# Closing batch 0's attention early in a fused attention and MLP kernel

## The chip, the cores and the metric

The kernel runs on one core of one Trainium2 chip. The metric is the device time of one execution in microseconds (us). An execution is called fast when it lies within 1.5% of the fastest of the same kernel, and a difference counts as faster or slower from 2% on. Ratios are the mean time of one kernel's fast runs over the mean of the other's in the same rounds, so they are not quite the ratio of the medians quoted beside them.

Engines: PE is TensorE (PEld its weight loads), DVE is VectorE, ACT is ScalarE, POOL is GpSimd, SP is SyncE. SPq and ACTq are queues on which SP and ACT issue transfers. TensorE's clock is called warm where 512-column products follow each other every 0.216 us, and cold where they do so every 0.42 us (five warming products).

## The reference

Eight batches, eight heads, 576 positions, head width 64; attention with a causal mask and a decay bias, then a normalisation over the 512 channels and an MLP of width 2048 with a residual.

```python
def _attn_ref(q, k, v, s):
    scores = scale * np.matmul(q, k.transpose(0, 1, 3, 2))
    cum = np.cumsum(np.maximum(s, 0.0), axis=-1)
    bias = -(cum[:, :, :, None] - cum[:, :, None, :])
    scores = np.where(causal, -1000000000.0, scores + np.minimum(bias, 0.0))
    # ... softmax ...
    return np.matmul(attn, v)

def _moe_ref(x, g_ln, w_ch1, w_ch2):
    mu = np.mean(x, axis=-1, keepdims=True)
    var = np.mean((x - mu) ** 2, axis=-1, keepdims=True)
    xn = (x - mu) / np.sqrt(var + 1e-06) * g_ln
    return x + np.maximum(xn @ w_ch1, 0.0) @ w_ch2
```

The bias enters as four more rows under the 64 rows of q and k (the "bias rows"), so that one product gives scores with bias.

## The kernel before

The 64 heads run in one loop. Head n's scores (q times k) are followed by the PV product (softmax weights times V) of an earlier head, and the MLP of batch b - 1 is cut into small units that fill TensorE while batch b's heads run. The PV result is drained by DVE. After a batch's last head, DVE aggregates the statistics and writes the normalised tiles `xn`; these are transposed on TensorE (`trx`) and copied to `xT`, from which the MLP starts.

```python
    def ln_aggr(b):
        n = len(x_tiles(b))
        mvs[b] = small.tile([P, 5, 2], F32, name="mv", tag="mv", bufs=2)
        for t in range(n):
            nc.vector.bn_aggr(out=mvs[b][:, t, :], in_=st[b][:, t, :, :])
    # ...
    def ln_xn(b):
        xTs[b] = xtp.tile([P, KD, 512], BF16, name="xT", tag="xT")
        for t, x in enumerate(x_tiles(b)):
            xn = xnp.tile([P, Dm], BF16, name="xn", tag="xn")
            nc.vector.scalar_tensor_tensor(
                out=xn, in0=x, scalar=mvs[b][:, t, 0:1], in1=gb,
                op0=ALU.subtract, op1=ALU.mult,
            )
            xns[b, t] = xn
    # ...
    def pv_next():
        pb, ph_ = pend.pop(0)
        pv(pb, ph_)
        if ph_ in (3, 5, 7):
            ln_stats(pb, ph_ // 2 - 1)
        if ph_ == 7:
            ln_aggr(pb)
            ln_xn(pb)
            ln_rstd(pb)
```

For the first three batches, k and q come in pairs of heads, are transposed on TensorE into PSUM (`trqk`) and copied from there (`qk_pair`). The loads that matter here stand in `pre(n)`, which runs ahead of head n. `ld_w1`, `ld_w2` and `ld_cast_pair` are issued by POOL, which also casts V:

```python
        elif n == 8:
            ld_cast_pair(6)
            ld_w2(1)
            cast_v(1, 0, "pool")
            cast_v(1, 1, "pool")
        elif n == 9:
            ld_w2(2)
            cast_v(1, 2, "pool")
            # ... V tiles 3 and 4
        elif n == 10:
            ld_cast_pair(7)
            ld_w2(3)
```

The softmax here doesn't subtract the row's maximum and nothing guards it: scores larger than these inputs give would overflow.

## Time and profile before

| | before |
|---|---|
| time, median (range) | 387.93 us (387.8 to 389.07), 3 runs |
| profiled span | 385.7 us |
| lost TensorE time, 0 to 50 us | 30.0 us |
| lost, 50 to 100 us | 7.2 us |
| lost, 310 to 320 us | 4.0 us |
| first MLP product | 45.53 us |
| head 63's scores begin | 299.78 us |

"Lost" is the length of the stretch less the columns of its matmuls at 2400 per us (narrow ones counted as 64), without the warming products; a product counts where it starts. It shows how far the stretch is from dense work, which busy time does not. The start of a head's first score product (`sa`) is a milestone: the same head in two kernels tells how far one is ahead. The main lines behind this table stand in the prediction.

### The profile page before, as it was taken

How to read it: one execution, taken by the hardware profiler on the slowest of the kernel's cores; microseconds unless marked ns; L12 is line 12 of the kernel's file. 1: busy time of each engine (PE TensorE's matmuls, PEld its weight loads, DVE VectorE, ACT ScalarE, POOL GpSimd, SP SyncE). 2: the span in 40 equal slices, each digit the busy share in tenths (PEclk: the TensorE clock that was granted, in tenths of full speed). 3: DMA queues.
4: the chain of work that ended last, by engine and by line, in shares of the span. 5: the costliest groups of instructions: out<-in, count | busy, mean ns of one | idle time of the engine just before them, and what ended most of it. 6: DMA issues, size and time to landing. Idle time of an engine off the chain costs nothing.

```text
span 385.7 us, 8249 instructions
## 1 busy us (share of the span) xinstructions
PE 363.9 (94%) x3016; PEld 197.3 (51%) x3016; DVE 202.5 (53%) x538; ACT 194.5 (50%) x366; POOL 161.6 (42%) x442
## 2 busy tenths in 40 slices
PE   7878798997999999999999999999999979999994
PEld 2556455555555555565555555555555534444442
DVE  7557747768644754484356536743665473212211
ACT  7768667673874377427733773376346401411410
POOL 5861377437473365535565563456742110000000
PEclk9889899999999999999999999999999989999999
DMA  8799996178795599759887996589620011002013
GB/s 199 126 182 195 210 168 128 24 167 166 165 186 121 129 229 202 169 132 216 185 202 184 204 191 163 140 200 210 152 97 0 2 56 54 1 29 82 0 34 77
DMA packets 147777, 51.86 MB, mean 134 GB/s; under 512 B 134140, under 2 KB 142936, under 8 KB 147736
## 3 DMA queue, kind: packets, MB, share of 16 engines
q1 hardware_dynamic: 139352, 44.18, 50.5%
q0 software_dynamic: 8384, 7.15, 12.2%
q8 instruction: 24, 0.39, 0.4%
q14 instruction: 17, 0.14, 0.1%
HBM read 37.11 MB, written 9.44 MB: 121 GB/s over the span
## 4 chain that ended last, share of the span: by engine, by line
PE 80%; DMA 8%; DVE 5%; ACT 3%; SPq 1%; issue 1%; POOL 0%; ACTq 0%; DVEq 0%; POOLq 0%
PE py L457 31%; PE ph L439 30%; DMA vtmp<-in_v_dram 7%; PE pot L352 6%; PE sc L276 3%; PE sb L276 3%; PE sa L276 3%; PE trx L426 2%; ACT er L287 2%; DVE xn L410 2%; ACT kq L96 1%; DMA pairtmp<-in_q_dram 1%; PE trqk L229 1%; DMA kq<-c 1%; DVE yo L466 1%
## 5 line engine op out<-in xcount | busy, mean ns | idle before, releaser
L457 PE MATMUL py<-w_bf,hT 128*128 128x512 bf16 x576 | 137.9, 381 | 2.5 <-DVE yo L466 2.2
L439 PE MATMUL ph<-xT,w_bf 128*128 128x512 bf16 x512 | 123.2, 382 | 1.2 <-DVE hT L447 1.0
L449 ACT ACTIVATE hT<-ph 128x512 bf16<-128x512 f32 x107 | 63.9, 598 | 85.5 <-PE ph L439 85.5
L439 PEld LDWEIGHTS <-w_bf 128*128 128x128 bf16 x576 | 52.0, 98 | 55.2 <-issue 6.0
L457 PEld LDWEIGHTS <-hT 128*128 128x128 bf16 x576 | 52.2, 98 | 52.8 <-issue 4.0
L287 ACT ACTIVATE er<-sa 128x512 bf16<-128x512 f32 x64 | 38.1, 596 | 71.6 <-PE sa L276 44.8
L295 POOL TENSOR_SCALAR_AFFINE_SELECT er<-er 128x128 bf16<-128x128 bf16 x216 | 58.4, 294 | 33.3 <-ACT er L287 33.3
L447 DVE TENSOR_SCALAR hT<-ph 128x512 bf16<-128x512 f32 x37 | 25.6, 691 | 58.0 <-PE ph L439 54.9
L163 POOL CAST rows<-rowtmp 128x512 bf16<-128x512 f32 (+1 forms) x50 | 30.4, 607 | 44.3 <-DMA rowtmp<-in_q_dram 39.9
L352 PEld LDWEIGHTS <-er 128*128 128x128 bf16 x960 | 38.3, 99 | 17.9 <-DVE xm L369 3.1
L276 PEld LDWEIGHTS <-kq 68*128 68x128 bf16 x440 | 32.8, 98 | 27.6 <-DMA kq<-c 2.5
L360 DVE RECIPROCAL rinv<-pot 128x5 f32<-128x5 f32 x64 | 12.4, 194 | 61.5 <-PE pot L352 61.3
L352 PE MATMUL pot<-v_bf,er 128*128 128x65 bf16 x960 | 40.6, 195 | 2.3 <-DVE xm L369 1.8
L287 ACT ACTIVATE er<-sc 128x512 bf16<-128x512 f32 x64 | 39.1, 611 | 0.0
L100 POOL CAST v_bf<-vtmp 128x512 bf16<-128x512 f32 (+1 forms) x40 | 24.6, 620 | 32.9 <-DMA vtmp<-in_v_dram 32.5
L287 ACT ACTIVATE er<-sb 128x512 bf16<-128x512 f32 x64 | 38.3, 598 | 0.0
L466 DVE SCALAR_TENSOR_TENSOR yo<-py,rstd,xb 128x512 f32<-128x512 f32 x32 | 23.8, 748 | 25.5 <-PE py L457 20.3
L96 ACT COPY kq<-trqk 64x576 bf16<-64x576 bf16 x28 | 22.5, 802 | 11.9 <-PE trqk L229 11.7
L362 DVE TENSOR_TENSOR xb<-pot,rinv 128x256 f32<-128x256 f32 x64 | 27.2, 425 | 2.2
L276 PE MATMUL sa<-kq 68*128 68x512 bf16 x64 | 24.6, 385 | 3.0 <-DMA kq<-c 2.4
L276 PE MATMUL sc<-kq 68*128 68x256 bf16 (+1 forms) x208 | 25.2, 232 | 0.2
L386 DVE BATCH_NORM_STATS2 stats<-xb 128x6 f32<-128x128 f32 (+1 forms) x96 | 25.0, 320 | 0.4
(93 smaller groups left out, 302.2 us busy)
## 6 DMA issues: line engine op xcount, KB each, us to landing
vtmp<-in_v_dram SPq DMA_DIRECT2D x32, 256.0 KB
out_dram<-yo SPq DMA_DIRECT2D x32, 256.0 KB
rowtmp<-in_k_dram SPq DMA_DIRECT2D x40, 128.0 KB
rowtmp<-in_q_dram SPq DMA_DIRECT2D x40, 128.0 KB
w_bf<-in_moe_w_ch_dram POOLq DMA_DIRECT2D x8, 512.0 KB, 11.1
kp<-in_k_dram POOLq DMA_DIRECT2D x10, 144.0 KB, 4.4
qp<-in_q_dram POOLq DMA_DIRECT2D x10, 144.0 KB, 5.1
vtmp<-in_v_dram SPq DMA_DIRECT2D x8, 128.0 KB
```

What stands on the lines that cost most here:

```text
L96: nc.scalar.copy(out=out, in_=in_)
L163: nc.gpsimd.tensor_copy(out=r[0:pn, :, :, 0:D], in_=loaded.pop(("rows", gam, t))[0:pn])
L276: nc.tensor.matmul(a[:, c + a0 - q0 : c + a1 - q0], lhsT=k_cols(b, h, kb), rhs=cols, start=True, stop=not (pe_mask and diag),)
L287: nc.scalar.activation(out=e[:, o : o + 512], in_=a, func=ACT.Exp, scale=scale)
L295: nc.gpsimd.affine_select(out=e[:, o : o + P], in_=e[:, o : o + P], compare_op=ALU.is_ge, fill=0.0, base=0, pattern=[[1, P]], channel_mult ...
L352: nc.tensor.matmul(pot[:, t, :], lhsT=e[:, o : o + P], rhs=vv[:, kb, h, :], start=(kb == 0), stop=(kb == last),)
L362: nc.vector.tensor_tensor(out=xb[b][:, :, hs], in0=pot[:, 0:NF, 0:D], in1=rinv[:, 0:NF].unsqueeze(2).to_broadcast([P, NF, D]), op=ALU.mult,)
L439: nc.tensor.matmul(ph, lhsT=w1_bf[:, kd, fb * P : (fb + 1) * P], rhs=xT[:, kd, :], start=(kd == 0), stop=(kd == KD - 1),)
L447: nc.vector.tensor_scalar_max(out=hT[:, fb, :], in0=ph, scalar1=0.0)
L449: nc.scalar.activation(out=hT[:, fb, :], in_=ph, func=ACT.Relu)
L457: nc.tensor.matmul(py[0], lhsT=hT[:, fb, t * P : (t + 1) * P], rhs=w2_bf[:, fb, :], start=(fb == 0), stop=(fb == FB - 1),)
L466: nc.vector.scalar_tensor_tensor(out=yo, in0=py[0], scalar=rs, in1=x, op0=ALU.mult, op1=ALU.add)
```

## The change

The intent is to begin the MLP sooner: batch 0's last three PV products are drained and normalised before batch 1 starts. The bias rows of the first heads come by broadcast transfer. Pair 1 no longer loads ahead of V. The end is shortened too. The core of the diff, cut:

```diff
@@ normalisation: one function for one tile, aggregate and xn in turn
-        for t in range(n):
-            nc.vector.bn_aggr(out=mvs[b][:, t, :], in_=st[b][:, t, :, :])
+    def ln_xn(b, t):
+        ...
+        nc.vector.bn_aggr(out=mvs[b][:, t, :], in_=st[b][:, t, :, :])
+        xn = xnp.tile([P, Dm], BF16, name="xn", tag="xn")
+        nc.vector.scalar_tensor_tensor(out=xn, in0=tiles[t], ...)
...
         if ph_ == 7:
-            ln_aggr(pb)
-            ln_xn(pb)
-            ln_rstd(pb)
+            ln_open(pb)
+            for t in range(NT if pb < B - 1 else 1):
+                ln_xn(pb, t)
@@ batch 0 closed after head 7
+            if n == 7:
+                pv_next()
+                tr_pair(4)
+                pv_next()
+                pv_next()
+                evac_pair("k", 4, ("act", "act"))
...
+        if n == 8:
...
+            for t in range(NF):
+                ln_tr(0, t, "act")
+            queue += batch_units(0)
+            run_units(3)
@@ loads
         elif n == 8:
-            ld_cast_pair(6)
             ld_w2(1)
-            cast_v(1, 0, "pool")
-            cast_v(1, 1, "pool")
         elif n == 9:
-            ld_w2(2)
-            cast_v(1, 2, "pool")
...
+            for t in range(NT):
+                cast_v(1, t, "pool")
+            ld_cast_pair(6)
         elif n == 10:
-            ld_cast_pair(7)
+            ld_w2(2)
             ld_w2(3)
...
+        elif n == 11:
+            ld_cast_pair(7)
@@ the end: last norm spread between units, its copies on ACT, last tile in halves
     for t in range(NT):
-        ln_tr(B - 1, t)
+        ln_xn(B - 1, t + 1)
         run_units(1)
+        ln_tr(B - 1, t, "act")
```

Not shown: the start's copies split over ACT and DVE, the transposes of the bias columns moved from head 14 to head 12 with half of their copies on ACT, pairs 7 to 10 transposed at heads 13 to 16, the PV product of head 7 in another PSUM buffer, and the number of MLP units per head, now computed from what is left in the queue.

## The prediction

> **What bounds the kernel now.** I read the page first, then the busy times by stage, then TensorE's waits, then the timeline where those waits stand. Of the page's slices (one is 9.64 us) these count:
>
> ```profile
> PE   7878798997999999999999999999999979999994
> ...
> PEclk9889899999999999999999999999999989999999
> DMA  8799996178795599759887996589620011002013
> ```
>
> TensorE is full from about 100 us to the end but for one dent near 315 us; the first five slices are 7s and 8s, and part of that is the kernel's own warming products. The stages, from the view by windows:
>
> ```profile
> 0.00:45.50 45.50, 35.00 (x370) 21.33 (x371) 31.26 (x82) 33.61 (x57) 23.46 (x44) 0.92 1.03 179
> 45.50:50.00 4.50, 4.13 (x28) 2.08 (x27) 0.69 (x1) 2.22 (x5) 2.29 (x5) 0.62 1.24 227
> ...
> 80.00:100.00 20.00, 17.69 (x170) 10.13 (x167) 14.24 (x39) 11.98 (x21) 11.68 (x32) 1.00 0.73 168
> 100.00:310.00 210.00, 209.92 (x1866) 116.59 (x1865) 115.56 (x333) 112.11 (x223) 104.10 (x312) 1.00 0.70 157
> 310.00:321.00 11.00, 8.75 (x48) 4.53 (x47) 7.18 (x19) 0.00 (x0) 1.16 (x1) 0.84 0.13 49
> ```
>
> The columns are PE, weight load, DVE, ACT, POOL, granted clock, DMA share, GB/s. Busy time flatters TensorE, so I count columns. Four 512-column products take 0.863 us in the timeline's dense stretches, 0.216 us each. In 0 to 45.5 us the products other than the 39 warming ones (groups by form) have 42,400 columns, 17.9 us at that rate: 27.6 us are lost. The same count gives 16.7 of 20 us in 80:100 (3.3 lost), 7.1 of 11 in 310:321 (3.9 lost), 8.1 of 10 in 60:70 (1.9 lost), and next to nothing in 100:310. So the total is TensorE's work plus these losses plus the tail. A loss removed comes off the end at full size, because everything after it is dense.
>
> Which waits are these? TensorE's waits in the first 130 us, longest first, are these (after 130 us one more counts: 2.2 us of py L457 for DVE yo L466, at 314.8 us):
>
> ```profile
> PE sa L276 <- DMA kq<-c: 2.4, 1, 2.4
> PE trqk L229 <- DVE xT L431: 2.1, 1, 2.1
> PE pot L352 <- DVE xm L369: 1.8, 2, 0.9
> PE trx L426 <- DVE xT L431: 1.7, 1, 1.7
> ```
>
> The first is head 4 waiting at 22.0 us for its bias rows; the clock then falls to half until 28.9 us. The second stands at 90.9 us: pair 10's transposes need a PSUM buffer that holds a transpose of batch 1's norm. Last, how the first MLP product is reached, and how the run ends:
>
> ```profile
> 38.20 0.64 PE L352 MATMUL pot<-v_bf,er 128*128 128x65 bf16 x15 [0.93 <-DVE xm L369]
> ...
> 40.20 3.26 ACT L96 COPY kq<-trqk 64x576 bf16<-64x576 bf16 x4 [2.12 <-PE trqk L229]
> ...
> 40.83 3.02 DVE L410 SCALAR_TENSOR_TENSOR xn<-xb,mv,gb 128x512 bf16<-128x512 f32 x4
> ...
> 43.84 1.64 DVE L431 COPY xT<-trx 128x512 bf16<-128x512 bf16 x4
> ...
> 45.53 1.55 PE L439 MATMUL ph<-xT,w_bf 128*128 128x512 bf16 x4
> ```
>
> ```profile
> 380.82 0.75 DVE L466 SCALAR_TENSOR_TENSOR yo<-py,rstd,xm 128x512 f32<-128x512 f32 x1 [2.70 <-PE py L457]
> 381.60 0.47 SPq L489 DMA_DIRECT2D out_dram<-yo  x1
> 382.12 0.59 SPq L490 DMA_DIRECT2D out_dram<-yo  x1
> ```
>
> Batch 0's last PV product starts at 38.2 us, and 7.3 us pass to the first MLP product: drain, statistics, four normalisations, then four copies on the same DVE. ACT meanwhile copies pair 5, and head 9's exponentials wait until 43.5 us.
>
> **What the Trainium skill says.** "Perfetto Trace Analysis", Identifying the Most-Contended Engine, says that matmul busy time is no measure of the distance to the roofline; the trace agrees (35.0 us busy, 17.9 us of columns). "TensorE: Matmul & The Clock Gate", What's actually happening, has the clock at half after an idle window of about 3.4 us; its section "Wait — 56ns, not 53.3ns?" puts 512 columns at 426.7 ns cold and 215.7 warm. The trace agrees: 0.216 us dense, and a granted clock of 0.62 in 45.5:50, just after the starved stretch. "DMA: Bandwidth & Descriptors", Anatomy of one DMA, has about 2.0 us of fixed cost per transfer. The first bias rows (4.5 KB or less) agree: last issue over at 11.7 us, used at 13.9. Its section Queues, rings and completion order has each engine alternate between queues by packet; so small rows queue with the weights, and the rows issued from 17.6 to 20.1 us landed only at 24.4.
>
> **The change part by part.**
>
> *Start.* Pair 1's k and q leave the first queue (two 288 KB loads), and the constant rows come by broadcast DMA in place of one 2.11 us ACT copy and the memsets. The first scores start at 12.14 us now. After it: k cast on ACT to 5.8, q cast on POOL (0.8 to 1.3 us) to about 7.2, then on ACT two k copies (0.81 each), the bias row (0.57) and two q copies. That gives about 10.4 us. The sync queue is blocked by V loads until 8.5 us now; with less ahead, the bias rows of heads 1 to 3 should land at about 13 us in place of 13.8. Gain at this point: about 1 us.
>
> *Heads 0 to 7.* Rows of group 1 are issued before the weights, so the 2.4 us wait goes, and most of the cold stretch behind it. ACT gets one q copy per pair in place of two (saves 0.8 us per pair), DVE three copies in place of two, so DVE becomes the pace-maker. From the first pair's copies to the last normalisation DVE has: 3 pairs x 3 x 0.81 = 7.3; 8 drains at 1.0 (0.20 + 0.42 + 0.27 and gaps) = 8.0; statistics 1.4 + 0.9 + 0.9 = 3.2; four times 0.12 + 0.74 = 3.4. Sum 21.9 us. From about 13.5 us that is 35.4 us at the earliest. Laying the steps out by hand in program order, with the one-buffer PV drain, gives scores 7 at 29, the last PV at 32.5, its drain over at 34.7, the last normalisation at 38.6, its ACT copy at 39.3, and the first MLP product at about 39.5 us against 45.53.
>
> *What that 6 us is worth.* By 50.0 us the old kernel has also done heads 9 and 10, pair 5, PV 8 and two MLP units: about 4.3 us of dense work (0.7 + 0.7 + 0.2 masks + 0.5 + 0.4 + 1.7 and small ones). The new one needs that too: 39.5 + 4.3 + about 2 for a cold clock = 45.8, against 50.0. Gain 4.2 us, the start included.
>
> *60 to 100 us.* No pair is transposed from n = 17 to 20, when batch 1's norm uses the same PSUM pool: the 2.1 us wait goes, and with it ACT's 3.25 us block at 79.95. I expect 2.5 of the 3.3 us lost in 80:100. The bias transposes move from n = 14 to 12, with half of their copies on ACT; of the 1.9 us in 60:70 I count 0.3.
>
> *Last norm.* Batch 7's five normalisations (2.67 + 0.74 us of DVE in one block) are spread between MLP units and the transposes copied by ACT, idle there (0.00 in the table). The outputs on DVE are no longer held up. Of 3.9 us I count 3.2.
>
> *Tail.* The last tile comes in two halves: the last output operation covers 256 columns (about 0.4 us by halving 0.75), and its two stores are issued on two queues, so 0.5 us less issuing. Gain 0.8. The 256-column products cost no more in sum: PV products with 65 columns already issue every 0.03 us.
>
> Sum: 4.2 + 2.8 + 3.2 + 0.8 = 11.0 us, 387.9 - 11.0 = 376.9 us.
>
> **The rivals.**
> 1. *DMA sets the pace instead.* The DMA row is full from 19 to 58 us, and V of batch 1 lands only at about 49. Against: the pair-6 load (0.29 MB), the gain broadcast (0.26 MB) and the third w2 load no longer compete with it. I count 4.7 MB from about 20 us; at 195 GB/s that ends near 45 us, and PV 8 is due near 49. For: V casts now wait for tiles four places later in the queue, and every weight load stands behind them on POOL. If V, or pair 5 behind four weight loads, is 3 us late, the prologue gains only 1.2 and the result is 380 us, at the border.
> 2. *DVE sets a later start than laid out.* Each drain waits behind three copies, and PV has one buffer. If this adds 3 us the result is again 380.
> 3. *Transposes bunched.* Pairs 7 to 10 at n = 13 to 16 put 1.6 us each on ACT and DVE in four steps of about 4.2 us. By then ReLUs are over (three units a head), so ACT has 3.3 us and DVE about 3.7. Tight; if it slips, the 2.8 us of the middle are lost: 379.7.
> 4. *Better than that.* If the clock stays warm into the first MLP products and the DVE chain overlaps better, the prologue gives 7 us: 374.
>
> **Range and chances.** The rivals are partly independent and mostly take 3 us each; two together would be needed to stay above the 2% border (380.2 us). The steps of the tail and the last norm (4.0 us) I hold nearly certain. So 376.9 us, with 371.5 to 382 for 8 in 10; faster by over 2%: 0.78; within: 0.20; slower: 0.02.
>
> **What would show it.** First scores near 10.5 us; no wait of sa for bias rows near 22; first MLP product at 38 to 41 us; PV 8 not waiting for V; no wait of trqk for xT near 90 us; 310:321's like with under 1 us lost; the last store issued within 0.7 us of the last product's output. An MLP start after 43 us, or a wait of over 2 us for V or pair 5, would make the prediction wrong.

## The result, and the profile after

| | before | after |
|---|---|---|
| time, median (range) | 388.1 us (387.8 to 389.07), 4 runs | 385.03 us (384.55 to 385.43), 4 runs |
| ratio | | 0.9916, 95% interval 0.9893 to 0.9939 |
| profiled span | 385.7 us | 383.6 us |
| lost, 0 to 50 us | 30.0 | 25.7 |
| lost, 50 to 100 us | 7.2 | 12.2 |
| lost, 310 to 320 us | 4.0 | 0.4 |
| first MLP product | 45.53 us | 39.72 us |
| head 21 begins | 101.21 us | 102.12 us |
| head 63 begins | 299.78 us | 302.54 us |
| from there to the end of the span | 85.9 us | 81.1 us |

The kernel gained about 3 us where 11 had been predicted. The prediction was wrong: 385.03 lies above its range. In the table the prologue (the stretch up to 50 us) gains 4.3 us; between 50 and 100 us 4.9 us are given back. Head 21 is 0.9 us behind the kernel before and head 63 is 2.8 us behind, so a further 1.9 us is lost between them; the end gains 4.8 us. The slices of the page first:

```profile
PE   7987887996999999999999999999999999999996
...
PEclk9999899999899999999999999999999999999999
DMA  8889979539992499949996999399950002002013
```

The dent near 315 us is gone. A new one stands in the tenth slice (86 to 96 us), and the granted clock dips in the eleventh. The view by windows, with the columns as before (PE, weight load, DVE, ACT, POOL, clock, DMA share, GB/s):

```profile
0.00:45.50 45.50, 37.54 (x374) 21.80 (x375) 28.68 (x79) 30.96 (x55) 21.24 (x43) 0.96 0.98 173
45.50:50.00 4.50, 4.50 (x27) 2.11 (x24) 1.48 (x3) 4.45 (x10) 1.67 (x3) 1.00 0.62 125
...
80.00:100.00 20.00, 16.43 (x159) 9.44 (x158) 14.40 (x39) 9.11 (x20) 12.38 (x35) 0.91 0.77 175
100.00:310.00 210.00, 209.21 (x1847) 115.58 (x1844) 117.83 (x327) 112.33 (x224) 105.38 (x317) 1.00 0.77 156
310.00:321.00 11.00, 11.00 (x80) 5.74 (x79) 8.69 (x22) 2.93 (x5) 1.16 (x1) 1.00 0.13 49
```

The stretch 80:100, in which 2.5 us were to be gained, now has 16.43 us of TensorE busy in place of 17.69 and a clock of 0.91. In 310:321 TensorE is busy throughout. Which waits of TensorE took the place of the old ones in the first 130 us:

```profile
PE pot L371 <- DVE xm L388: 3.2, 4, 1.8
PE trqk L237 <- DMA kp<-in_k_dram: 2.4, 2, 1.8
...
PE trx L447 <- DVE xT L99: 1.2, 1, 1.2
```

The columns are total us, how often, and the longest. The 2.4 us wait for bias rows is gone, as is the wait of pair 10 on the norm's buffers. In their place stand a PV product behind DVE (1.8 us at once, ended at 92.80 us) and pair loads that had not landed. The MLP's start itself went as laid out:

```profile
31.85 1.09 PE L371 MATMUL pot<-v_bf,er 128*128 128x65 bf16 x30 [0.42 <-DVE xm L388]
...
36.76 1.17 ACT L97 COPY xT<-trx 128x512 bf16<-128x512 bf16 x2
...
39.72 1.87 PE L460 MATMUL ph<-xT,w_bf 128*128 128x512 bf16 x6 [0.67 <-ACT xT L97]
```

ACT copies `xT` while DVE still normalises (its last tile from 37.84 us), and the first MLP product comes 5.8 us sooner. The late pair is seen in the timeline at head 13:

```profile
54.08 0.64 POOL L128 DMA_DIRECT2D qp<-in_q_dram  x1
...
64.28 0.43 PE L237 MATMUL trqk<-ident,kp 96*128 96x96 bf16 x6 [1.78 <-DMA kp<-in_k_dram]
...
65.19 0.43 PE L237 MATMUL trqk<-ident,qp 96*128 96x96 bf16 x6 [0.48 <-DMA qp<-in_q_dram]
```

The first line is the issue, the others are the products that wait for it. This transfer of 0.29 MB was issued on the same queue behind two weight loads of 1.05 MB each (128 x 4 x 512 values of 4 bytes), and the chain of waits gives it 11.07 us from 54.08. Pair 6, behind V's casts, costs 0.59 and 0.39 us in the same way at 52.6 us: V's last cast had itself waited 2.83 us for its transfer and began at 48.84, and pair 6 was issued from 49.40.

The third new cost is on DVE. Batch 1's norm, first in the kernel before:

```profile
85.05 0.60 DVE L398 BATCH_NORM_AGGREGATE mv<-stats 128x2 f32<-128x18 f32 x5
85.56 2.67 DVE L410 SCALAR_TENSOR_TENSOR xn<-xb,mv,gb 128x512 bf16<-128x512 f32 x4
88.15 0.74 DVE L410 SCALAR_TENSOR_TENSOR xn<-xm,mv,gb 128x512 bf16<-128x512 f32 x1
```

and then in the changed one:

```profile
86.96 0.22 DVE L427 BATCH_NORM_AGGREGATE mv<-stats 128x2 f32<-128x18 f32 x1
87.22 0.75 DVE L429 SCALAR_TENSOR_TENSOR xn<-xb,mv,gb 128x512 bf16<-128x512 f32 x1
...
90.95 0.75 DVE L429 SCALAR_TENSOR_TENSOR xn<-xm,mv,gb 128x512 bf16<-128x512 f32 x1
```

In a block, five aggregates take 0.60 us together and the normalisations follow one another every 0.65 us or so, overlapping at their ends: from 85.05 to the next instruction at 88.81 is 3.76 us, 0.75 a tile. In turn, each aggregate takes 0.22 us by itself and its reader starts only after it: from 86.96 to the next at 91.62 is 4.66 us, 0.93 a tile. TensorE's next PV product needs its buffer drained by DVE, which comes behind this block:

```profile
92.80 0.62 PE L371 MATMUL pot<-v_bf,er 128*128 128x65 bf16 x15 [1.77 <-DVE xm L388]
...
95.10 0.48 PE L447 MATMUL trx<-ident,xn 128*128 128x128 bf16 x4 [1.23 <-DVE xT L99]
...
96.65 1.91 PE L460 MATMUL ph<-xT,w_bf 128*128 128x512 bf16 x4
```

It waits 1.77 us, the transposes of the norm wait 1.23 us after it, and the scores and four MLP products from 95.37 to 98.36 us then run at the cold clock (0.43 us a product).

At the end of the run the two halves and two queues are seen:

```profile
373.73 7.15 SPq L512 DMA_DIRECT2D out_dram<-yo  x4
373.73 7.18 ACTq L513 DMA_DIRECT2D out_dram<-yo  x4
...
379.90 0.48 DVE L487 SCALAR_TENSOR_TENSOR yo<-py,rstd,xm 128x256 f32<-128x256 f32 x1 [1.26 <-PE py L478]
```

The last output operation takes 0.48 us in place of 0.75, and both stores are issued by 380.9 us, 0.5 us after it.

### The profile page after: what moved, and what is told of

Same layout as the page of the kernel before. It is cut to its first block, busy times and chain, and to the rows that moved or that the text cites. A ratio compares the mean times of both kernels' runs of the same rounds, so it can differ in the third digit from the quotient of the medians.

```text
span 383.6 us, 8277 instructions
## 1 busy us (share of the span) xinstructions
PE 363.9 (95%) x3028; PEld 197.2 (51%) x3028; DVE 204.5 (53%) x531; ACT 194.5 (51%) x371; POOL 160.4 (42%) x442
## 4 chain that ended last, share of the span: by engine, by line
PE 57%; DMA 16%; SPq 7%; POOL 6%; DVE 6%; issue 5%; ACT 2%; POOLq 0%; ACTq 0%
PE py L478 23%; PE ph L460 22%; DMA vtmp<-in_v_dram 8%; PE pot L371 4%; SPq L152 3%; DMA rowtmp<-in_q_dram 3%; DMA qp<-in_q_dram 3%; SPq L135 2%; PE sb L294 2%; PE sc L294 2%; PE sa L294 2%; DVE xn L429 2%; POOL er L313 1%; POOL v_bf L101 1%; DMA kq<-rows 1%
## 5 line engine op out<-in xcount | busy, mean ns | idle before, releaser
L478 PE MATMUL py<-w_bf,hT 128*128 128x512 bf16 (+1 forms) x592 | 136.8, 373 | 0.6 <-DVE yo L487 0.6
L478 PEld LDWEIGHTS <-hT 128*128 128x128 bf16 x592 | 53.4, 98 | 49.0 <-issue 1.1
L371 PEld LDWEIGHTS <-er 128*128 128x128 bf16 x960 | 37.4, 98 | 19.1 <-DVE xm L388 2.5
L421 POOL TENSOR_TENSOR rstd<-rstd,mhalf 128x4 f32<-128x4 f32 (+1 forms) x8 | 8.8, 1096 | 51.6 <-DVE rstd L420 51.5
L99 DVE COPY kq<-trqk 64x576 bf16<-64x576 bf16 x23 | 18.1, 801 | 14.2 <-PE trqk L237 14.0
```

Of the source, the lines that this page charges most:

```text
L371: nc.tensor.matmul(pot[:, t, :], lhsT=e[:, o : o + P], rhs=vv[:, kb, h, :], start=(kb == 0), stop=(kb == last),)
L478: nc.tensor.matmul(py[0], lhsT=hT[:, fb, t * P : (t + 1) * P], rhs=w2_bf[:, fb, c0:c1], start=(fb == 0), stop=(fb == FB - 1),)
```

## The experiments

All outputs are right.

The kernel before took 387.81, 387.51 and 388.69 us (medians) in the three calls, so kernels of different calls are best compared by their ratios.

| kernel | median us (range) | ratio to before, 95% interval |
|---|---|---|
| changed, first time | 385.03 (384.55 to 385.43) | 0.9916 (0.9893 to 0.9939) |
| changed, again | 384.02 (381.54 to 385.6) | 0.9891 (0.9849 to 0.9933) |
| tail alone | 383.62 (381.96 to 385.87) | 0.9894 (0.9859 to 0.9928) |
| aggregates in a block | 380.0 (378.54 to 382.68, and one of 1314.16) | 0.9804 (0.9768 to 0.984) |
| the same, again | 380.46 (378.57 to 381.96) | 0.9792 (0.976 to 0.9824) |
| pairs loaded sooner | 381.31 (378.99 to 384.18) | 0.9834 (0.9796 to 0.9872) |
| both of these | 379.16 (377.31 to 380.83) | 0.979 (0.9761 to 0.9819) |
| both, batch 0 closed late | 381.26 (380.08 to 382.08) | 0.9829 (0.9795 to 0.9864) |
| both, norms spread | 379.4 (377.95 to 379.97) | 0.9776 (0.9741 to 0.981) |
| best | 375.71 (375.19 to 377.8) | 0.9694 (0.9658 to 0.9731) |
| best, bias copies split again | 375.67 (374.26 to 378.24) | 0.9681 (0.9649 to 0.9713) |
| best, transposes on DVE again | 376.85 (376.03 to 380.65) | 0.973 (0.969 to 0.977) |
| best, weights early again | 377.41 (376.21 to 378.54) | 0.9721 (0.9694 to 0.9747) |

**Aggregates in a block.** The changed kernel with the five aggregates of batches 0 to 6 in one block again; batch 7 stays spread.

```diff
+        if b < B - 1:
+            for t in range(len(x_tiles(b))):
+                nc.vector.bn_aggr(out=mvs[b][:, t, :], in_=st[b][:, t, :, :])
...
-        nc.vector.bn_aggr(out=mvs[b][:, t, :], in_=st[b][:, t, :, :])
+        if b == B - 1:
+            nc.vector.bn_aggr(out=mvs[b][:, t, :], in_=st[b][:, t, :, :])
```

> The changed kernel with the five aggregates of batches 0 to 6 in one block again (batch 7 stays interleaved). Theory A: an aggregate just ahead of the normalisation that reads it costs DVE a bubble (0.93 us a tile in place of 0.75 to 0.8), and the longer block is what lets TensorE lose 0.2 to 0.7 us at four later batches; then heads 35 to 56 lose no more against the kernel before (1.9 us in the changed kernel), and batch 1's close is some 0.7 us shorter: 2 to 3 us faster than the changed kernel, near 382.5 us. Rival: the later losses come from the new spreading of MLP units; then the block changes less than 0.5 us.

Its fast runs gain 3.4 to 4.3 us on the changed kernel's (ratio 0.9804 against 0.9891 and 0.9916), more than the 2 to 3 us expected. The profiled execution was the one of 1314.16 us, and its trace can't be compared, so the kernel was run again.

> The kernel with the change, whose five aggregates of batches 0 to 6 stand in one block again, a second time (the first one's profile fell on an execution at a quarter of TensorE's speed). Theory D (aggregate and normalisation in turn hold up the MLP's outputs in every batch): batch 1's block of statistics and normalisations ends 3.8 us after it begins in place of 4.7, the steps from head 35 to 36 and from 55 to 56 are 5.3 and 4.6 us in place of 5.8 and 5.3, and the median is 379 to 381. Rival (the first run's gain was chance of the clock at the MLP's start): these steps stay at 5.8 and 5.3, and the median is 383 to 385.

The second run confirms both the time (380.46 us) and the mechanism. By chance its heads agree with those of the changed kernel's profile to 0.02 us from head 16 (78.47 and 78.49 us) to head 18 (84.56 and 84.57), so the two traces can be laid over each other:

```profile
86.95 0.60 DVE L417 BATCH_NORM_AGGREGATE mv<-stats 128x2 f32<-128x18 f32 x5
87.47 2.67 DVE L433 SCALAR_TENSOR_TENSOR xn<-xb,mv,gb 128x512 bf16<-128x512 f32 x4
90.05 0.74 DVE L433 SCALAR_TENSOR_TENSOR xn<-xm,mv,gb 128x512 bf16<-128x512 f32 x1
```

The block begins 0.01 us apart and ends 0.90 us sooner (90.72 against 91.62). Head 20 then begins at 94.42 in place of 95.37, head 21 at 99.55 in place of 102.12: 0.9 us of DVE became 2.6 us of TensorE. Of these 0.9 us is the longer wait itself (1.77 us for the drain, against 0.69 here), and 1.6 us the cold stretch that followed it, which this trace does not have. The rest comes later, at 35 to 36 (5.24 us against 5.77), 51 to 52 and 55 to 56 (4.57 against 5.28): there the norm holds up the MLP's output `yo` on DVE (in the changed kernel TensorE waits 0.36 us for it at 169.32). At head 63 the difference is 4.33 us, the same as between the spans (379.3 and 383.6). The second run's rival, chance at the MLP's start, falls, because these steps came out as the theory had said. So does the first run's, the new spreading of MLP units: from head 21 to 63 this kernel takes 198.66 us with the new spreading, the kernel before 198.57 with the old.

**Pairs loaded sooner.** Pair 6 is loaded at head 8, ahead of V's casts, and pair 7 at head 9, ahead of the last two weight loads.

```diff
         elif n == 8:
             ld_w2(1)
+            ld_cast_pair(6)
         elif n == 9:
             for t in range(NT):
                 cast_v(1, t, "pool")
-            ld_cast_pair(6)
+            ld_cast_pair(7)
...
         elif n == 11:
-            ld_cast_pair(7)
```

> The changed kernel with pair 6 loaded at step 8 ahead of the V casts and pair 7 at step 9 ahead of the last two w2 loads. Theory B: TensorE's 3.3 us of waits for these two pairs (52.0 to 53.4 and 62.5 to 65.2 us) move everything after them; then head 16 starts about 3 us earlier and the end comes 2.5 to 3.5 us earlier, near 382 us. Rival C: batch 0's MLP units run out before batch 1's norm is ready, so a gain at head 13 is given back as a longer hole near 90 us; then the end moves by under 1 us though head 13 is 2 us or more earlier.

The waits for the pair loads are gone; pair 7's product no longer carries one in the timeline:

```profile
61.15 0.42 PE L237 MATMUL trqk<-ident,kp 96*128 96x96 bf16 x6
61.52 0.42 PE L237 MATMUL trqk<-ident,qp 96*128 96x96 bf16 x6
```

Against the changed kernel the ratio falls by 0.006 to 0.008, 2 to 3 us. Part of the gain in this one profile is a warmer MLP start (8.3 us from head 8 to 9 in place of 10.0), so the waits alone are worth less than the difference of the profiles. The rival falls: head 13 begins 3.7 us earlier than in the changed kernel, and head 63 6.5 us earlier, so nothing was given back.

This run also shows what the aggregates in turn cost without late pairs, for it still has them. From head 18 to 20 it takes 10.74 us, as the changed kernel does (10.80, and 10.90 again) and against 9.86 with the block. But the cold stretch is not there (head 20 to 21 in 5.13 us, against 6.74 and 8.15), and from head 21 to 63 it takes 199.31 us against 200.42 and 200.29, and 198.66 with the block. So the turns by themselves cost 0.9 + 0.7 us in the traces; the rest of what the block saved was a loss that only the two runs of the changed kernel show, with turns and late pairs together.

**Both of these.**

> Both edits. If A and B hold and are independent, the gains add: 4.5 to 6.5 us faster than the changed kernel, 378.5 to 380.5 us. If C holds, no better than the aggregate block alone by more than 1 us.

The two gains do not add up: 379.16 us is 0.8 us under the blocked aggregates (380.0; ratios 0.979 and 0.9804), and 1.7 us by the ratios under the pairs loaded sooner (0.9834). By the ratios, then, each repair is worth less on top of the other than by itself, and by rival C's own measure, 1 us, the medians don't exclude it. The traces do: this one is 3.8 us ahead of the second run of the block at head 63. Of that, 1.8 us is already there at head 8, where the two have the same code behind them, which is chance; the other 2.0 us come between heads 8 and 13, where the pairs were late, and are kept from there on (head 13 to 63 takes 232.72 and 232.79 us). With both causes removed, the changed kernel is 8.65 us faster than before (387.81 - 379.16); 2.35 us are still missing to the 11.0 predicted.

**Tail alone.** The kernel before, with only the end of the change: last norm spread, transposes copied by ACT, last tile in halves on two queues.

> The kernel before with only the end of the change: batch 7's normalisations spread between MLP units, its transposes copied by ACT, the last tile in two halves on two queues. Prediction's terms: 3.2 + 0.8 = 4.0 us; the two traces give 4.9 us between head 63 and the end. So 383 to 384 us, which is faster than the whole change: then all else in the change is a net loss of 1 to 2 us. If the end is worth under 2 us, the rest of the change is not a loss and theory A and B have less to explain.

It takes 383.62 us, as much as the whole change. From head 63 to the end of the span it needs 80.9 us, against 85.9 before and 81.1 with the whole change, so the end is worth 5.0 us alone. All of the change's net gain is thus its end; its other parts came to about zero together.

**The changed kernel again.**

> The changed kernel as it is, run beside the next three so that they compare on one chip. Ratio to the kernel before 0.992 as on record, near 384.7 us; head 20 starts about as late as in the kernel before (within 1.5 us), head 63 later than in the kernel before by 1 to 3 us.

A median of 384.02 us confirms the result. In its profile head 20 to 21 takes 8.1 us on a cold clock (granted 0.50 in 96:100), so the stretch behind batch 1's norm is lost there too. Head 63 is 2.9 us behind the kernel before, as expected; head 20 is 1.7 us ahead of it, just outside what was expected.

**Batch 0 closed late.** Both repairs, with the PV products and the MLP's start at the heads of the kernel before.

```diff
-        if n < 8:
+        if n < 10:
...
+            if n == 9:
+                for t in range(NF):
+                    ln_tr(0, t, "act")
+                queue += batch_units(0)
```

> The kernel with both repairs, but batch 0 closed as in the kernel before: its last products at steps 8 and 9, MLP from step 10. Theory D: most of the prologue's gain is the start and the early bias rows (3.6 us at head 7 in the changed kernel), and closing early only moves idle time, because heads 9 to 19 then run under the same limits of V loads, DVE and ACT with fewer MLP units each; then this is 0 to 1.5 us slower than with both repairs (379 to 380.5 us). Rival, the prediction's own account: the early MLP start is worth most of the 6 us; then this is 3 us or more slower (382 us or more).

It is slower than with the early close by 0.0039 of before's time (0.9829 - 0.979): 1.5 us, at the upper end of theory D's 0 to 1.5 and far from the rival's 3. That is about what the early close is worth once both repairs are in. The two intervals overlap a little, so the size is rough.

**Norms spread.** Both repairs, and for batches 1 to 6 the last three normalisations moved behind the next batch's first PV drain.

```diff
-            for t in range(NT if pb < B - 1 else 1):
+            for t in range(NT if pb == 0 else 2 if pb < B - 1 else 1):
                 ln_xn(pb, t)
...
+        if b > 1 and h == 2:
+            for t in range(2, NT):
+                ln_xn(b - 1, t)
```

> Both repairs, and for batches 1 to 6 the last three normalisations moved behind the next batch's first drain on DVE. Theory E: near 84 to 91 us TensorE waits for the drain and the copies that stand behind the block of five (2.75 us lost in 80:90 with both repairs); with the block cut the drain comes 2 us earlier and 1 to 1.5 us of that loss goes: 377.5 to 378.2 us. If the loss is the shortage of MLP units (6 left for three heads), it only moves: within 0.5 us of both repairs.

379.4 us against 379.16, ratios 0.9776 and 0.979: nothing to be seen, and theory E's 1 to 1.5 us did not come. In the trace head 18 to 20 takes 10.19 us, against 9.85 with both repairs alone: the loss near 90 us only moved, as the expectation's other branch has it. TensorE's wait for the drain (0.68 us) is gone, and its waits for the copies of the norm's transposes grew from 1.23 to 1.83 us.

**A better version.** On top of the last one: all four loads of the second weight behind V's casts of batch 1, the bias columns copied by DVE alone, and batch 1's transposes copied by ACT.

```diff
-        elif n == 7:
-            ld_w2(0)
         elif n == 8:
-            ld_w2(1)
             ld_cast_pair(6)
...
         elif n == 10:
+            ld_w2(0)
+            ld_w2(1)
+        elif n == 11:
             ld_w2(2)
             ld_w2(3)
...
-            nc.scalar.copy(out=cT[0:pn, t0:t1, 1, :, 0], in_=tr[0:pn, 0, t0:t1, :])
+            nc.vector.tensor_copy(out=cT[0:pn, t0:t1, 1, :, 0], in_=tr[0:pn, 0, t0:t1, :])
...
-            ln_tr(b - 1, t)
+            ln_tr(b - 1, t, "act" if b == 2 else "dve")
```

> Spread, and: all four w2 loads behind the V casts of batch 1 (TensorE waited 1.4 us for V's last cast with both repairs), the bias columns copied by DVE alone (in the changed kernel ACT and DVE take turns on one PSUM tile, 2.7 us of waits), batch 1's transposes copied by ACT. About 1 us from the first, 0.5 us from each of the others: 375.5 to 377.5 us. If w2 then comes late, the first py products near 62 us wait and it is no better than spread.

375.71 us, 0.9694 of before: it beats both kernels clearly, and reaches the time that had been predicted for the change, though with edits that the prediction did not have. Which of the three additions did it was asked by taking each away.

> The best kernel, but with batch 1's transposes copied by DVE, as the changed kernel has them. Theory H (DVE holds the transposes' buffers while it still normalises): TensorE waits 1 us or more for xT between 90 and 100 us, and the median is 0.5 to 1 us above best's. Rival: within 0.4 us of best.

1.1 us slower in the median, 1.4 by the ratios, and the trace shows why: the wait for the copy of the norm's transposes is back (in 40 to 100 us).

```profile
PE trx L451 <- DVE xT L99: 1.8, 2, 1.4
```

Head 18 begins at 79.92 us (80.13 with the copies on ACT), head 21 at 95.01 (93.73). This addition is confirmed, with 1.5 us in the trace.

> The best kernel, but with the copies of the bias columns split between ACT and DVE, as the changed kernel has them. Theory G (ACT and DVE take turns on one PSUM tile, and head 12's exponentials stand behind it): waits of 0.5 to 1.5 us in the copies between 57 and 62 us come back, and the median is about 1.3 us above best's, 376.5 to 377.5. Rival: within 0.5 us of best.

No difference (375.67 us; 0.9681 against 0.9694). The wait that was expected does come back (1.49 us of ACT on DVE in the copies), but heads 8 to 13 take 25.93 us against 25.85. That theory falls: the same wait of 1.49 us in the changed kernel's profile, too, is then likely to have cost next to nothing.

> The best kernel, but with the four loads of the second weight ahead of V's casts of batch 1, as the changed kernel has them. Theory F (the casts wait behind these loads, PV 8 waits for V, and the MLP's beginning stays cold): the last cast of V of batch 1 near 49 us in place of 44, PV 8 waits over 1 us, and the median is about 2 us above best's, 377.5 to 378.5. Rival (best's gain comes from the bias columns): within 0.7 us of best, whose median should be near 375.7.

1.7 us slower in the median, 1.0 by the ratios. V's last cast begins at 49.79 us in place of 44.23, as expected, but PV 8 follows head 10 by 2.45 us in both, so the wait that was to be the mechanism is not there. What the two traces do show is that this one was 1.7 us behind at head 2 already (18.44 us against 16.70), before the first of the moved loads was issued at 25.83, 1.8 us at head 8, and 1.3 us at head 63. So in these two traces the lag comes from the clock at the start. Two warming products after head 1's scores, first in the best kernel, then here:

```profile
15.72 0.59 PE L535 MATMUL idle<-zeros 128*128 128x512 bf16 x2
```

```profile
17.58 1.05 PE L535 MATMUL idle<-zeros 128*128 128x512 bf16 x2
```

The code up to there is the same; in one execution TensorE was warm by 14 us, in the other it is still cold at 17.6. Whether that also accounts for the medians of six runs isn't shown, and what the place of these loads is worth stays open. So of the 3.7 us between the spread kernel and the best one, 1.1 to 1.5 are shown to be the transposes on ACT, none is the bias columns, and the rest isn't settled.

## Why the prediction was wrong

- **First scores.** Predicted near 10.4 us, measured 12.35. ACT's last q copy ends at 11.06 us and DVE's last bias row at 11.2, because ACT waited 0.59 us for a bias product. And five warming products of 512 columns that stand ahead of the scores ran at the cold clock from 10.24 us: the scores follow when they are through. The prediction's account of the start doesn't mention them. The 2 us did no harm later: heads 0 to 7 had been priced by DVE's work from 13.5 us on.
- **Heads 0 to 7 and the MLP's start.** Right. Scores 7 at 29.04 us for 29, first MLP product 39.72 us for about 39.5, PV 8 not waiting for V, no wait for bias rows; the gain counted up to 50 us is 4.3 us (30.0 - 25.7) for 4.2, "the start included". So close a hit is partly luck, as the start gave nothing of its 1 us. One term was off without harm then: "four times 0.12 + 0.74" took the aggregate's time from a block, where in turn a tile costs 0.93 us.
- **60 to 100 us.** This is the step that failed. "I expect 2.5 of the 3.3 us lost in 80:100" and "of the 1.9 us in 60:70 I count 0.3", together 2.8 us gained; from 60 to 100 us the kernel lost 3.1 us more than before (9.8 against 6.7), and from 50 to 60, for which nothing was counted, 1.8 us more (2.3 against 0.6). Two things stood in the diff and were not weighed. The pair loads had moved behind V's casts and weight loads on POOL's queue; loading them sooner is worth 2 to 3 us by itself (on top of the other repair, about 2.0 in the traces and 0.5 by the ratios). And the aggregates, now in turn with their readers, made batch 1's norm 0.9 us longer just where a PV product waits behind it, which TensorE paid with 2.6 us, 1.6 of it on a cold clock. The wait that the prediction had looked at did go, and others took its place. Its own list shows the gap: of the signs that it named, all but the first scores' came true, and TensorE met neither of the two that were to make it wrong; the list watched no pair but pair 5, and not how long DVE's norm took.
- **The dense part.** The prediction took 100 to 310 us as untouched ("a loss removed comes off the end at full size, because everything after it is dense"). The rule itself held: the pairs' 2.0 us were kept from head 13 to the end. But the tile-by-tile norm applies to every batch; it cost another 1.8 us between heads 21 and 63 (4.33 - 2.57 in the laid-over traces), though only 0.7 us where the pairs were not late. Taking turns thus cost about 4 us as the change stood, the largest single error, and 1.6 to 1.7 us of that with the pairs in time (0.9834 - 0.979, and 0.9 + 0.7 in the traces). Why late pairs make turns dearer isn't shown. The reading "next to nothing in 100:310" was generous: the count there gives 5.8 us of 210 before, with TensorE busy for 209.92.
- **Last norm and tail.** Right in kind, and mis-sized: predicted 3.2 + 0.8 = 4.0 us, measured 4.8 in the changed kernel and 5.0 alone. The 310:320 loss went from 4.0 to 0.4, which is 0.4 more than counted.
- **The rivals.** The first had the right place, loads behind others on POOL, and V of batch 1 did come at about 49 us (last cast at 48.84), but it named V and pair 5 as what TensorE would wait for; pairs 6 and 7 were late. The third, transposes bunched at heads 13 to 16, named the middle's gain as lost, but by the wrong means: from 70 to 80 us 0.7 us were lost, as before. The rivals were mostly given 3 us each; the stretch from 50 to 100 us alone fell short by 7.7 us (2.8 + 4.9).
- **The sum of it.** With both causes repaired the kernel takes 379.16 us, inside the predicted range, 8.65 us less than before. Of these the early close is worth 1.5 us and the end 5.0 (alone, by the trace); the other 2 us or so weren't separated by a run. That the repaired kernel lands in the range doesn't make the prediction right: it needs two edits that the change didn't have.

## What to carry to other kernels

When a loop over tiles is rewritten to do "statistic, then its reader" per tile, look at what the block form cost: here short vector operations in a row overlapped (0.75 us a tile), and a reader directly behind its writer did not (0.93). A change that is meant for one batch but edits a function which all batches use must be priced once per batch. And when loads are reordered on one queue, list what each consumer now stands behind: here a transfer of 0.29 MB, issued behind two of 1.05 MB, was waited for until 65 us, 11 us after its issue.

## What the Trainium skill lacked or had wrong

- "VectorE: DVE Perf Modes", The DRAIN you can't avoid, measures eight copies in a row with and without a semaphore after each and finds that the semaphore costs nothing extra. It has no figure for a reader directly behind its writer. Here that order does cost: five aggregates and five normalisations took 3.76 us as two blocks and 4.66 us in turn, 0.18 us more a tile.
- "TensorE: Matmul & The Clock Gate", Seeing it yourself, mentions a clock stuck at a quarter for 50 us and more. One execution here was about that slow throughout: a span of 1312.3 us, four 512-column products in 3.36 us (0.84 us each, against 0.216), while the record gave the granted clock as 1.000. The record's clock doesn't show this state; the spacing of the products does.
- The same page, What's actually happening, says that the point of warming up varies by about 500 ns from run to run. That figure is for products back to back; here there are gaps between them, and the difference was larger: with the same code up to there, the cold products of the start ended at 13.6 us in one execution and at 18.4 us in another, and head 2 began 1.7 us apart. So a difference of that size between two single traces can be chance.
